# Gated layer: output weights made during its first half, products in another order, and the channel stage's operands and weights loaded one step ahead

## The chip, the cores and the metric

The kernel runs on one core of one Trainium2 chip. The metric is the device time of one execution in microseconds (us), as the median of several runs.

## The reference, cut to what matters

Three layers follow one another, all in float32: attention over 4 batches of 12 heads (448 positions, 64 channels a head), a gated layer (768 to 1024 channels and back), and a mixer that works first over the positions (448 to 256 and back) and then over the channels (768 to 1536 and back).

```python
scores = cap * np.tanh(scale * np.matmul(q, k.transpose(0, 1, 3, 2)) / cap)
attn = np.exp(scores - max); attn = attn / (attn.sum(-1) + 1e-09); x = np.matmul(attn, v)
...
h = np.maximum(x @ w_in, 0.0)                       # gated layer, 768 -> 1024
conv = sum(conv_w[k] * hp[:, k:k + S, :] for k in range(3))
x = h * (1 / (1 + np.exp(-conv))) @ w_out           # 1024 -> 768
...
h = np.maximum(x.transpose(0, 2, 1) @ w_tok1, 0.0) @ w_tok2
u = x + h.transpose(0, 2, 1)
out = u + np.maximum(u @ w_ch1, 0.0) @ w_ch2        # 768 -> 1536 -> 768
```

## The kernel before

Nearly every matrix product is made of three TensorE passes: each float32 operand is split into a rounded high part and the low rest (a cast on ScalarE and a subtraction on VectorE), and `split3` pairs high with high, high with low and low with high. The weights come as float64 words; `narrow` loads such words into `w_raw`, turns them into float32 (one ScalarE pass, three VectorE passes in `w_pt`) and splits them. All transfers are issued on one queue, that of SyncE (SP).

A list scheduler orders each engine's instructions by priority, which is the order of the program text moved by the offsets of `later(...)`, and puts a wait where an instruction needs one; each engine then works through its list in that order. A tile of a pool is taken over when all users of the tile that had its place are done.

**Attention and gated layer.** The loop over `gi` makes one quarter of a head pair's attention at a time. From the second batch on, the gated layer of the batch before is woven in: `gated(b)` is a generator, and each of its `yield`s names a cost that is charged against a budget (`RATES`). Its first half makes, for each of 8 blocks `m`, 18 products with `win[m]` (L466), then the gate on ScalarE and VectorE (L469 to L481), which leaves `gs[m] = (gh, gl)`. Its second half makes, for each of 6 output blocks `m`, 24 products over 8 values of `k` (L492) with the weight tile `wo[b, m]`, evacuates them (L496) and writes `y_d`. `wo` has two buffers of 1 MB. For the first batch (b = 0) `make_wo` narrows each tile from the words in three pieces (L352 to L366) and keeps a copy in `wo_d` (L427); for the other three, `load_wo` reads that copy in one transfer (L435). Here `load_wo(b, 0)` and `load_wo(b, 1)` stand at the start of the second half, and `load_wo(b, m + 1)` at the start of block `m`. One `w_raw` and one `w_pt` buffer of the pool `st` serve, one piece after another, `w_in` (16 pieces), then `w_out` (18 pieces), then `w_ch2` (24 pieces, L504).

**Tokens.** `tokens(b)` transposes `y_d` (L701), splits it (L703 to L707), makes the products over the positions (L718, L732), adds (L734) and writes `u_d` (L735). The steps of batches 0 to 2 are woven into the last batch's `gated`; the rest runs in a loop of its own, `while toks`.

**Channels.** The product `u @ w_ch1` is made by a Strassen-like scheme of seven products a unit (`up`, L873), whose right-hand operands `u0` to `u6` (`BORDER`) are sums and differences of four tiles of `u_d`, split again (L790, L791; the subtractions are L798). `u_make(p, k, want)` loads four tiles (L795) and makes those operands whose names are in `want`. For the first pair of batches, `u_all(0, BORDER[0:3])` makes three kinds during `while toks`, every second step; the other four kinds are made after that loop, from the same tiles loaded again. A step's four loads stand directly ahead of what uses them. The left-hand operands come from `w_ch1` blocks, one for each `wc_step`: `block` loads the words and narrows them at once (L635). `down` makes the second product (L911) with `w2` tiles, of which two lie in the pool `Gm` and two in `Gb`; `Gb` is opened when the tokens' pools are closed.

Of the kernel before, what the change touches and what calls it, by code (L numbers as in the profile page):

```python
# [20 lines left out]
KD = DM // 128  # L21
# [12 lines left out]
W_IN = 5  # L34
W_OUT = 7
# [13 lines left out]
WCK = 3  # L49
RATES = 13.0, 11.5, 13.0, 12.0  # L50
# [253 lines left out]
def fused_kernel(ctx, tc, ins, out, attention):  # L304
# [154 lines left out]
    def gated(b):  # L459
        gs = []  # L460
        for m in range(MF):
            hi, lo = win[m]
            ps = ps_m.tile([128, 512], F32, name="mm")
            for k in range(KD):
                for n, (w, v) in enumerate(split3(hi[:, k], lo[:, k], *X[b, k])):
                    nc.tensor.matmul(ps[:, 0:S], w, v, start=k == 0 and n == 0, stop=k == KD - 1 and n == 2)  # L466
                if k % 2 and k < KD - 1:
                    yield W_IN
# [13 lines left out]
            yield W_IN  # L482
        load_wo(b, 0)
        for m in range(KD):
            if m + 1 < KD:
                load_wo(b, m + 1)
            w = wo.pop((b, m)).rearrange("p t (k n) -> p t k n", n=128)
            hi, lo = w[:, 0], w[:, 1]
            ps = ps_m.tile([128, 512], F32, name="mm")
            for k in range(MF):  # L490
                for n, (w, v) in enumerate(split3(hi[:, k], lo[:, k], *gs[k])):
                    nc.tensor.matmul(ps[:, 0:S], w, v, start=k == 0 and n == 0, stop=k == MF - 1 and n == 2)  # L492
# [135 lines left out]
    def block(pools, src, name):  # L628
# [3 lines left out]
        raw = raw()  # L632
        p = pool.tile([128, 2, 384], U32, name="w_pt")[:, 0]
        t = blk.tile([128, 384], U32, name=name)
        nc.sync.dma_start(raw.rearrange("p n t -> p (n t)"), src)  # L635
# [3 lines left out]
    def unit_jobs(u):  # L639
# [9 lines left out]
        def a11(pools):  # L649
            T["a"] = block(pools, src(0, 0), "ba")  # L650
            put("A11", T["a"])

        def a21(pools):
            T["b"] = block(pools, src(1, 0), "bb")
# [4 lines left out]
        def a22(pools):  # L659
            t = block(pools, src(1, 1), "bx")  # L660
# [7 lines left out]
        def a12(pools):  # L668
            t = block(pools, src(0, 1), "bx")
# [4 lines left out]
        return [a11, a21, a22, a12]  # L674
# [94 lines left out]
    Gb = None  # L769

    def u_tile(o, k):
        name = BORDER[o]
        if o < 3:
            t = Gm.tile([128, 2, S], F32R, name=f"u{o}{k}", tag=f"u{o}{k}")
        elif name == "T4":
            t = Gb.tile([128, 2, S], F32R, name=f"u{o}{k}", tag=f"u{o}{k}")
# [247 lines left out]
```

## Time and profile before

| | |
|---|---|
| runs | 903.06 us median of 3 (899.55 to 904.08) |
| profiled execution | 902.45 us, its span 900.6 us |
| TensorE busy | 867.5 us, 96% of the span |
| VectorE, ScalarE busy | 696.1 and 495.5 us (77% and 55%) |
| granted TensorE clock, mean | 0.991 of full |

The span runs from the first to the last instruction of the profiled execution; the 1.85 us beside it lie around it. A TensorE instruction can overlap the next, so its busy time counts from the start of one to the end of a run of them; idle time stands in brackets or after a bar, with the instruction or transfer that ended it.

### The profile page before, as it was taken

The numbers are of one execution on the slowest core, as the hardware profiler recorded it, in microseconds if no ns is written. First come the engines' busy times: TensorE is split into PE (matmuls) and PEld (weight loads), VectorE is DVE, ScalarE is ACT, GpSimd is POOL, SyncE is SP. The second block draws the span as 40 slices with busy tenths as digits, with TensorE's granted clock in tenths as the row PEclk, the third lists the DMA queues.
The fourth block names the chain that finished last, engine by engine and source line by source line (L and its number), as shares of the span: only waits on it lengthen the run. The fifth ranks groups of instructions, "written<-read, shape, count | busy, mean of one in ns | idle before, by whom it ended". The sixth has DMA issues, their size and how long they took to land.

```text
span 900.6 us, 12120 instructions
## 1 busy us (share of the span) xinstructions
PE 867.5 (96%) x4105; PEld 754.4 (84%) x4105; DVE 696.1 (77%) x1271; ACT 495.5 (55%) x820; POOL 4.7 (1%) x19
## 2 busy tenths in 40 slices
PE   8999999989989999999999998999999999999997
PEld 4665887868978889888989988789989899999996
DVE  7889987789997899956897576796967859478342
ACT  6889888767886779863764243442423423143110
POOL 0000000000000000000000000000000000000000
PEclk9999999999999999999999999999999999999999
DMA  7875564667557864457658766556473744517234
GB/s 277 268 219 171 170 201 147 208 210 243 162 177 265 283 219 145 132 181 263 219 162 258 245 199 199 157 176 195 123 245 96 224 151 126 182 55 224 76 109 140
DMA packets 81719, 168.91 MB, mean 188 GB/s; under 512 B 12050, under 2 KB 57586, under 8 KB 79346
## 3 DMA queue, kind: packets, MB, share of 16 engines
q1 hardware_dynamic: 81650, 168.07, 58.1%
q8 instruction: 34, 0.56, 0.3%
q14 instruction: 35, 0.29, 0.1%
HBM read 126.58 MB, written 38.54 MB: 183 GB/s over the span
## 4 chain that ended last, share of the span: by engine, by line
PE 54%; DVE 19%; DMA 15%; ACT 7%; issue 4%; SPq 1%; POOL 0%; DVEq 0%; ACTq 0%; POOLq 0%
PE mm L911 18%; PE o L873 14%; PE mm L492 9%; DMA w_raw<-in_w_in 3%; DMA w_raw<-in_w_out 2%; DMA c<-u_d 2%; PE mm L466 2%; PE ps_e L718 2%; PE ps_e L732 2%; DMA w_d<-w_pt 1%; DVE ab L115 1%; DMA raw<-in_qk 1%; PE ps_s L147 1%; DVE w_pt L358 1%; PE ps_s L146 1%
## 5 line engine op out<-in xcount | busy, mean ns | idle before, releaser
L911 PE MATMUL mm<-hs,w 128*128 128x448 f32 x864 | 178.4, 367 | 0.8 <-DVE rr L912 0.7
L911 PEld LDWEIGHTS mm<-hs,w 128*128 128x128 f32 x864 | 161.7, 188 | 16.2 <-DVE rr L912 1.4
L492 PE MATMUL mm<-gh,wo 128*128 128x448 f32 x384 | 127.1, 374 | 6.4 <-ACT wo L362 3.4
L466 PE MATMUL mm<-xx,wi_h 128*128 128x448 f32 x384 | 114.7, 370 | 0.2 <-DVE xx L453 0.2
L492 PEld LDWEIGHTS mm<-gh,wo 128*128 128x128 f32 x384 | 72.8, 190 | 17.2 <-ACT wo L362 5.4
L146 PE MATMUL ps_s<-ab 128*128 128x448 f32 x192 | 81.6, 426 | 2.9 <-DVE ab L115 2.1
L466 PEld LDWEIGHTS mm<-xx,wi_h 128*128 128x128 f32 x384 | 71.7, 188 | 9.2 <-issue 1.9
L168 ACT ACTIVATE a<-ps_s,icap 128x896 f32<-128x896 f32 x76 | 67.0, 885 | 22.4 <-PE ps_s L147 17.9
L492 PE MATMUL mm<-gl,wo 128*128 128x448 f32 x192 | 71.2, 371 | 0.4 <-DVE gl L481 0.4
L147 PE MATMUL ps_s<-low,ab 128*128 128x448 f32 x192 | 71.3, 373 | 0.3 <-DVE low L116 0.3
L169 ACT ACTIVATE a<-a,cap 128x896 f32<-128x896 f32 x76 | 70.4, 926 | 1.3
L466 PE MATMUL mm<-xx,wi_l 128*128 128x448 f32 x192 | 70.3, 366 | 0.0
L176 DVE TENSOR_TENSOR al<-a,ah 128x896 fp32r<-128x896 f32 (+1 forms) x56 | 54.3, 971 | 1.7
L873 PE MATMUL o<-u,wi_h 128*128 128x448 f32 x216 | 49.4, 363 | 1.4 <-ACT u L790 1.1
L790 ACT CAST u<-c 128x448 fp32r<-128x448 f32 x48 | 27.0, 567 | 42.5 <-DVE c L798 21.9
L873 PE MATMUL o<-u,wi_l 128*128 128x448 f32 x216 | 47.9, 362 | 0.0
L146 PEld LDWEIGHTS ps_s<-ab 128*128 128x128 f32 x192 | 36.3, 190 | 13.4 <-issue 5.0
L175 DVE CAST ah<-a 128x896 fp32r<-128x896 f32 (+1 forms) x56 | 31.5, 565 | 18.9 <-PE ob L196 9.6
L873 PEld LDWEIGHTS o<-u,wi_h 128*128 128x128 f32 x216 | 40.5, 188 | 5.1 <-ACT u L790 1.9
L147 PEld LDWEIGHTS ps_s<-low,ab 128*128 128x128 f32 x192 | 36.4, 190 | 9.0 <-issue 5.4
L873 PEld LDWEIGHTS o<-u,wi_l 128*128 128x128 f32 x216 | 40.5, 187 | 2.7
L111 ACT CAST ab<-raw 128x960 fp32r<-128x960 f32 x36 | 35.4, 992 | 12.3 <-DMA raw<-in_qk 7.1
(166 smaller groups left out, 1690.5 us busy)
## 6 DMA issues: line engine op xcount, KB each, us to landing
wo<-wo_d SPq DMA_DIRECT2D x18, 1024.0 KB
raw<-in_qk SPq DMA_DIRECT2D x18, 960.0 KB
w_raw<-in_w_ch SPq DMA_DIRECT2D x40, 384.0 KB
c<-u_d SPq DMA_DIRECT2D x60, 224.0 KB
w_raw<-in_w_in SPq DMA_DIRECT2D x16, 384.0 KB
e<-in_qk SPq DMA_DIRECT2D x6, 960.0 KB
y_d<-c SPq DMA_DIRECT2D x24, 224.0 KB
yt<-y_d SPq DMA_DIRECT2D x24, 224.0 KB
```

The lines of the kernel that those rows point to most:

```text
L111: nc.scalar.copy(h, r)
L146: nc.tensor.matmul(ps[:, bank, 0:S], a[:, keys], a[:, 0:S], start=start, stop=False)
L147: nc.tensor.matmul(ps[:, bank, 0:S], a[:, keys], low, start=False, stop=stop)
L168: nc.scalar.activation(a[:, 0:n], ps[:, 0:n, 0:S], AF.Tanh, scale=self.c["icap"])
L169: nc.scalar.activation(a[:, 0:n], a[:, 0:n], AF.Exp, scale=self.c["cap"])
L175: nc.vector.tensor_copy(ah[:, 0:n], a[:, 0:n])
L176: nc.vector.tensor_tensor(al[:, 0:n], a[:, 0:n], ah[:, 0:n].bitcast(F32), op=ALU.subtract)
L466: nc.tensor.matmul(ps[:, 0:S], w, v, start=k == 0 and n == 0, stop=k == KD - 1 and n == 2)
L492: nc.tensor.matmul(ps[:, 0:S], w, v, start=k == 0 and n == 0, stop=k == MF - 1 and n == 2)
L790: nc.scalar.copy(w[:, 0], t)
L873: nc.tensor.matmul(ps, l, r, start=k == 0 and n == 0, stop=k == 2 and n == 2)
L911: nc.tensor.matmul(ps[:, 0:S], l, x, start=r == 0 and n == 0, stop=r == 3 and n == 2)
```

## The change

The second half's first two weight tiles are asked for at blocks 5 and 7 of the first half, in every batch; each later tile `m + 2` is asked for when block `m` is done. For the three later batches the first two output blocks are made together: `k` = 0 to 6 of block 0, `k` = 0 to 6 of block 1, and then `k` = 7 of both. For the first batch the yields cost 4 in the first half and 8 in the second, where all batches had 5 and 7; the sum of a batch's yields stays 288. In the channel stage, `u_begin` makes the first pair's operands in two groups (four kinds, then three) with each step's four loads issued one step earlier, alternately into the tiles `c` and into four tiles that are idle by then (`temp`); the first group runs at odd steps below 20 of `while toks`, the second from step 17 of the last batch's tokens on. T3 moves to `Gm`, T4 to the pool `xe`, and all four `w2` tiles to `Gb`. `wc_step` issues the words of the next `w_ch1` block before it narrows this one. `up` takes its four temporaries at once, in another order.

```diff
-W_IN = 5
-W_OUT = 7
+PACE = (4, 8), (5, 7)
+WO_AT = 5, 7
+UB_AT = 20, 17
...
     def gated(b):
         gs = []
+        w_in, w_out = PACE[b > 0]
         for m in range(MF):
+            if m in WO_AT:
+                load_wo(b, WO_AT.index(m))
...
-        load_wo(b, 0)
-        for m in range(KD):
-            if m + 1 < KD:
-                load_wo(b, m + 1)
-            w = wo.pop((b, m)).rearrange("p t (k n) -> p t k n", n=128)
...
-                if k % 2 and k < MF - 1:
-                    yield W_OUT
+        def mm(m, k):
+            if k == 0:
+                acc[m] = ps_m.tile([128, 512], F32, name="mm")
+            w = wo[b, m].rearrange("p t (k n) -> p t k n", n=128)
+            for n, (l, v) in enumerate(split3(w[:, 0, k], w[:, 1, k], *gs[k])):
+                nc.tensor.matmul(acc[m][:, 0:S], l, v, start=k == 0 and n == 0, stop=k == MF - 1 and n == 2)
+
+        def done(m):
+            del wo[b, m]
             y = cv_p.tile([128, S], F32, name="c", bufs=4)
-            nc.scalar.activation(y, ps[:, 0:S], AF.Copy, scale=0.5)
+            nc.scalar.activation(y, acc.pop(m)[:, 0:S], AF.Copy, scale=0.5)
             nc.sync.dma_start(y_d[b, m], y)
-            yield W_OUT
+            if m + 2 < KD:
+                load_wo(b, m + 2)
+
+        blocks = [[(0, k) for k in range(MF - 1)] + [(1, k) for k in range(MF - 1)] + [(0, MF - 1), (1, MF - 1)]] if b else [[(m, k) for k in range(MF)] for m in range(2)]
+        blocks += [[(m, k) for k in range(MF)] for m in range(2, KD)]
+        n = 0
+        for m, k in (i for l in blocks for i in l):
+            mm(m, k)
+            if k == MF - 1:
+                done(m)
+            n += 1
+            if n % 2 == 0:
+                yield w_out
...
     def wc_step(pools, n=1):
         for _ in range(n):
             if todo:
                 with later(tc, O_NA):
-                    todo.pop(0)(pools)
+                    for words, _ in todo[len(ahead) : 2]:
+                        ahead.append(fetch(pools, words))
+                    todo.pop(0)[1](ahead.pop(0))
...
+    def u_first(k, b11, b12, b22, b21):
+        u_put(k, "B11", b11)
+        sub(b11, b12, b11)
+        yield
+        sub(b12, b22, b12)
+        sub(b22, b22, b11)
+        u_put(k, "T2", b22)
+        yield
+        u_put(k, "B21", b21)
+        u_put(k, "T3", b12)
+        yield
+
+    def u_rest(k, b11, b12, b22, b21):
+        sub(b11, b12, b11)
+        sub(b12, b22, b11)
+        sub(b21, b12, b21)
+        u_put(k, "T4", b21)
+        yield
+        u_put(k, "T1", b11)
+        u_put(k, "B22", b22)
+        yield
+
+    def u_begin():
+        steps = [(u, i) for u in (u_first, u_rest) for i in range(3)]
+        ts = u_load(0, 0, 0)
+        yield
+        for n, (u, i) in enumerate(steps):
+            coming = u_load(0, steps[n + 1][1], (n + 1) % 2) if n < 5 else None
+            yield from u(i, *ts)
+            ts = coming
...
-        if k % 2:
-            next(first, None)
+        n += 1
+        left += len(toks) == 1
+        if n % 2 and n < UB_AT[0] or left >= UB_AT[1]:
+            next(begin, None)
...
-        pool = Gm if c % 4 < 2 else Gb
-        w2[c] = w = pool.tile([128, 2, KD * 128], F32R, name=f"w2_{c % 4}", tag=f"w2_{c % 4}")
+        w2[c] = w = Gb.tile([128, 2, KD * 128], F32R, name=f"w2_{c % 4}", tag=f"w2_{c % 4}")
...
-        p1, u2 = temp(), temp()
+        p1, c21, u3, u2 = (temp() for _ in range(4))
...
-    for _ in u_all(0, BORDER[3:7]):
-        pass
```

## Rows read from the trace of the kernel before

**Rows 1.** The page: engines over the span, and the longest group of products.

```profile
PE 867.5 (96%) x4105; PEld 754.4 (84%) x4105; DVE 696.1 (77%) x1271; ACT 495.5 (55%) x820; POOL 4.7 (1%) x19
L911 PE MATMUL mm<-hs,w 128*128 128x448 f32 x864 | 178.4, 367 | 0.8 <-DVE rr L912 0.7
```

**Rows 2.** TensorE's groups from 176 to 216 us, idle time and releasers last.

```profile
L492 PE MATMUL mm<-gh,wo 128*128 128x448 f32 x35 | 12.1, 386 | 4.2 <-ACT wo L362 3.4 <-DVE wo L366 0.7
```

**Rows 3.** TensorE in order of time, first batch: first and last of three waits.

```profile
179.36 0.47 PE L492 MATMUL mm<-gh,wo 128*128 128x448 f32 x1 [1.38 <-ACT wo L362]
...
212.02 0.47 PE L492 MATMUL mm<-gh,wo 128*128 128x448 f32 x1 [1.01 <-ACT wo L362]
```

**Rows 4.** All users of `wo`: min/median/max ns, first and last start in us.

```profile
L492 PE MATMUL mm<-gh,wo x384: 358/367/742, 138.7 to 522.7; 128*128 128x448 f32 x192
...
L362 ACT CAST wo<-w_pt x18: 396/502/517, 110.4 to 218.0; 128x384 fp32r<-128x384 f32 x12, 128x256 fp32r<-128x256 f32 x6
```

**Rows 5.** Transfers of `w_out` pieces in order of time on SP: first, eighth, ninth.

```profile
99.63 0.33 SPq L352 DMA_DIRECT2D w_raw<-in_w_out  x1
...
143.18 0.33 SPq L352 DMA_DIRECT2D w_raw<-in_w_out  x1
...
153.72 0.33 SPq L352 DMA_DIRECT2D w_raw<-in_w_out  x1
```

**Rows 6.** TensorE's waits over the span: us in total, times, longest.

```profile
PE mm L492 <- ACT gh L480: 1.2, 2, 1.1
```

**Rows 7.** TensorE in order of time around the second batch's turn.

```profile
260.73 0.36 PE L492 MATMUL mm<-gh,wo 128*128 128x448 f32 x1
...
268.42 0.47 PE L197 MATMUL oa<-al,v 128*128 128x448 f32 x1 [1.42 <-DVE al L176]
269.97 0.74 PE L492 MATMUL mm<-gh,wo 128*128 128x448 f32 x1 [1.08 <-ACT gh L480]
```

**Rows 8.** SP, ACT and PE in order of time, last batch's tokens.

```profile
542.98 9.94 SPq L795 DMA_DIRECT2D c<-u_d  x8
...
547.09 0.56 ACT L790 CAST u<-c 128x448 fp32r<-128x448 f32 x1 [1.87 <-DMA c<-u_d]
...
548.08 0.62 PE L718 MATMUL ps_e<-xx,wt 128*128 128x384 f32 x2 [2.73 <-ACT xx L703]
```

**Rows 9.** PE and DVE in order of time, start of the channel stage.

```profile
560.02 1.97 PE L873 MATMUL o<-u,wi_h 128*128 128x448 f32 x9
...
565.16 0.62 DVE L798 TENSOR_TENSOR c<-c 128x448 f32<-128x448 f32 x1 [3.30 <-DMA c<-u_d]
```

**Rows 10.** TensorE's groups from 552 to 575 us, idle time and releasers last.

```profile
L873 PE MATMUL o<-u,wi_h 128*128 128x448 f32 x23 | 6.0, 372 | 1.0 <-ACT u L790 0.8 <-DVE u L791 0.3
L873 PE MATMUL o<-xx,wi_l 128*128 128x448 f32 x12 | 4.1, 479 | 1.2 <-ACT xx L790 1.2
```

**Rows 11.** By stretch: window, length, engines' busy us, clock, DMA share, GB/s.

```profile
80.00:140.00 60.00, 59.51 (x251) 46.30 (x250) 53.19 (x104) 52.14 (x86) 1.96 (x6) 1.00 0.54 173
180.00:200.00 20.00, 17.21 (x73) 13.87 (x73) 18.00 (x30) 13.26 (x21) 0.63 (x1) 0.91 0.60 194
260.00:280.00 20.00, 17.50 (x78) 15.06 (x77) 16.24 (x29) 15.53 (x24) 0.00 (x0) 0.91 0.63 204
284.00:304.00 20.00, 20.00 (x100) 18.01 (x99) 15.37 (x26) 15.83 (x23) 0.00 (x0) 1.00 0.83 292
560.00:580.00 20.00, 17.79 (x78) 15.56 (x78) 14.60 (x26) 7.40 (x14) 0.00 (x0) 0.91 0.55 170
```

**Rows 12.** SP in order of time: the second batch's second weight tile.

```profile
226.88 0.33 SPq L435 DMA_DIRECT2D wo<-wo_d  x1
```

**Rows 13.** The chain that ended last, at the end of the third batch.

```profile
410.76 5.77 DMA wo<-wo_d
```

**Rows 14.** TensorE's groups from 284 to 304 us.

```profile
L492 PE MATMUL mm<-gh,wo 128*128 128x448 f32 x37 | 12.1, 366 | 0.0
L492 PE MATMUL mm<-gl,wo 128*128 128x448 f32 x19 | 6.9, 364 | 0.0
```

More of the change, by code (lines that the diff above doesn't have):

```diff
@@ L467, in gated @@
                 if k % 2 and k < KD - 1:
-                    yield W_IN
+                    yield w_in
             h = hb[m % 2]
@@ L481, in gated @@
             nc.vector.tensor_tensor(gl, c, gh.bitcast(F32), op=ALU.subtract)
[L482 to L494 removed]
+            yield w_in
+        acc = {}
+        def mm(m, k):
[6 more added lines that the diff above has]
+            del wo[b, m]
             y = cv_p.tile([128, S], F32, name="c", bufs=4)
[L496 removed]
+            nc.scalar.activation(y, acc.pop(m)[:, 0:S], AF.Copy, scale=0.5)
             nc.sync.dma_start(y_d[b, m], y)
[L498 removed]
+            if m + 2 < KD:
[10 more added lines that the diff above has]
+                yield w_out
     def w2_early(c, i):
@@ L806, in u_make @@
         yield
-        if "T3" in want:
-            sub(b12, b22, b12)
-            put("T3", b12)
-        sub(b22, b22, b11)
-        put("T2", b22)
-        yield
-        if "T4" in want:
-            sub(b21, b22, b21)
-            put("T4", b21)
-        yield
-    def u_all(p, want):
-        for k in range(3):
-            yield from u_make(p, k, want)
+        u_put(k, "B21", b21)
[10 more added lines that the diff above has]
+        yield
@@ new lines, in u_begin, with u_all @@
+    def u_begin():
[6 more added lines that the diff above has]
+            ts = coming
+    def u_all(p):
+        for k in range(3):
+            b11, b12, b22, b21 = u_load(p, k)
+            u_put(k, "B11", b11)
+            sub(b11, b12, b11)
+            u_put(k, "T1", b11)
+            yield
+            u_put(k, "B21", b21)
+            u_put(k, "B22", b22)
+            yield
+            sub(b12, b22, b12)
+            u_put(k, "T3", b12)
+            sub(b22, b22, b11)
+            u_put(k, "T2", b22)
+            yield
+            sub(b21, b22, b21)
+            u_put(k, "T4", b21)
+            yield
@@ L822, in fused_kernel, with temp @@
+    spare = [0]
+    def temp():
+        spare[0] = i = (spare[0] + 1) % 4
+        if i < 2:
+            return cv_p.tile([128, S + 2], F32, name=f"h{i}", tag=f"h{i}")[:, 0:S]
+        name = ("sums", "rr")[i - 2]
+        return pools["sm"].tile([128, S], F32, name=name, tag=name)
     toks.append(tokens(B - 1))
-    first = u_all(0, BORDER[0:3])
+    begin = u_begin()
+    n = left = 0
     while toks:
@@ L829, in fused_kernel @@
             wc_step(st_pools)
-        if k % 2:
-            next(first, None)
-    for _ in first:
+        n += 1
+        left += len(toks) == 1
+        if n % 2 and n < UB_AT[0] or left >= UB_AT[1]:
+            next(begin, None)
+    for _ in begin:
         pass
```

74 lines of the change are left out of this document (32 added, 42 removed).

## The prediction

> **What bounds the kernel now.** I read the page first: TensorE is busy for 867.5 us, 96% of the span, the next engine for 77% [rows 1]. So the change can give back only what TensorE stands idle, and what its clock loses after standing. Second come its waits and its groups by stretch, which say where it stands; third the timelines of the queue or engine named there, which say why. What the reader should see are three places.
>
> The first is the first batch's second half. In 40 us L492 stands 4.2 us, all of it for pieces of `wo` still being narrowed [rows 2], at three points of the same look, 14 to 18 us apart (the middle one is left out) [rows 3]. The pieces were not asked for late: the first was cast at 110.4 us and the first product ran at 138.7 [rows 4]. They come through one `w_raw` and one `w_pt` buffer. The 18 transfers start at 99.63; the ninth starts 10.5 us after the eighth, where those before came every 6.2 us ((143.18 - 99.63) / 7) [rows 5]. The tile they fill takes the place of tile 0, whose products are running then. So this chain, not the program's order, is what is late.
>
> The second is the turn in the later batches: L492 waited for the last gate block 1.2 us in all, 1.1 of it once [rows 6], at 269.97, just after an attention wait of 1.42 [rows 7].
>
> The third is the end of the tokens. Eight loads of `u_d` drag over 9.94 us on SP, ScalarE reaches a cast of theirs 1.87 us before its load lands, the tokens' own copies stand behind that cast, and TensorE stands 2.73 us [rows 8]. Then three products' worth of operands are ready and the fourth's are not: VectorE waits 3.30 us for another load [rows 9], and L873 stands 1.0 and 1.2 us [rows 10].
>
> The clock adds to each: 0.91 over the 20 us of 180 to 200, 260 to 280 and 560 to 580, 1.00 in the other stretches shown [rows 11]. Either level is 2.4 or 1.2 GHz, so each of these stretches lost 20 x (1 - 0.91) = 1.8 us, each after waits of over 2 us within a few us.
>
> **Operands one step ahead.** The number of loads (24), casts (21) and VectorE passes stays; only their place moves. Each step's four loads stand a whole step (three calls) before their use, so the cast no longer meets its own load, and the copies behind it go through. T3 joins the first group: four products instead of three are ready at the start, 9 passes more at 0.20 us (100 in 20 us) [rows 11], 1.8 us of cover, and the second group begins while the tokens' last products run. What goes: 2.73 + 1.0 + 1.2 and the dip after it, 1.8: 6.7 us. Bounds: 0 (the casts still block) to 6.7. I take it whole, as the waits named are on the loads themselves and on what queued behind them. VectorE has room for it (14.6 of 20 us) [rows 11]. What is late next is T4 and T1 in `xe`, whose nine places the tokens' copies hold until their last block; the 1.8 us of cover is theirs.
>
> **First batch.** The change lets `load_wo(0, 0)` and `(0, 1)` with all their work (six transfers in, six out, 12 ScalarE and 24 VectorE passes) stand at an earlier place, and moves a later tile by one yield. The transfers in cannot start before 99.63, because `w_in` has the buffers until then; but the passes get their turn sooner, and the pace (4 for 5, then 8 for 7) brings tile 0 to its end sooner, so the 10.5 us gap, 4.3 over the others, shrinks; and it spreads the second half over 192 / 168 of the steps. Against this, block 5 is needed earlier too. Bounds of the gain: 0, and 4.2 + 1.8 = 6.0 us. I take half, 3.0, since the chain gains some 4 us and loses part of it to the earlier need. The pace has a bound on the other side: in 80 to 140 VectorE carries 53.2 of 60 us [rows 11]; squeezed by a fifth throughout, that work would be 53.2 - 48 = 5.2 us late. Only the gate's part is squeezed, and the attention of the steps left out goes with it, so I put nothing and keep 5 us for the range.
>
> Of the rule that repeated gaps can mean too few buffers (the Trainium skill, Perfetto Trace Analysis, Identifying the Most-Contended Engine and Optimization Strategy), this trace gives an instance, three gaps of one kind in 33 us [rows 3], and the change adds no buffer. By the rule the first batch would give 0 instead of 3.0; that is the second rival below.
>
> **Later batches, first two tiles.** Asked for sooner, but the second batch's second tile is issued at 226.88 [rows 12], and its first product runs at 260.73 [rows 7]: 33.8 us of slack hide an earlier or later issue. A transfer of 1 MB takes 5.77 us [rows 13]. So 0 here; if that cover were gone, 5.8. SP's other transfers stand behind such an issue when it waits for its place; the same slack pays.
>
> **Later batches, new order.** With block 1 between, the last gate block has 21 more passes to arrive, 4.3 us; the 1.2 us of [rows 6] go. The dip at 270 follows 1.42 and 1.08 us of waiting; one of these goes, so I count half of 1.8. Together 2.1; bounds 0 and 3.0.
>
> **Its cost.** Tile 2 takes tile 0's place. Before, it was asked for with all of block 1 to run. Now block 0 ends three passes (0.6 us) before block 1, and block 2 comes at once: of 5.77 us, 5.2 are bare in each of three batches, and tile 3 is in flight beside it. What can cover them is attention. At 284 to 304 us 56 of 100 passes are L492's [rows 14], 44 attention's, and ScalarE is busy 15.83 of 20 [rows 11], so attention could run at most 20 / 15.83 = 1.26 times as fast and fill 0.44 x 1.26 = 0.55 of the time. That leaves 0.45 x 5.2 = 2.3 us. Bounds: 0, when the scheduler finds enough, and 3 x (5.2 + 1.8) = 21.0, all bare and a dip each. I take 2.3 in the second and third batch and nothing in the fourth, where three batches' token products stand ready: 4.6 us.
>
> For 1 MB the Trainium skill (DMA: Bandwidth & Descriptors, Bandwidth) has 6.15 us, measured on another issuing path; the row here has 5.77. By the page the bare time would be 5.55 and the term 5.0, a sum later by 0.4.
>
> **At nothing.** Words one block ahead: the transfers feed `up`, and in the whole of L911's 178.4 us TensorE idles 0.8 [rows 1]. The temporaries' order: within the same 0.8. `w2` in `Gb`: first used after two `up`s, 126 passes or 25 us. If these covers fail, what is lost is at most a late transfer, as the 5.77.
>
> **Sum.** 902.45 (span 900.6 and 1.85 around it) - 6.7 - 3.0 - 2.1 + 4.6 = 895.2. The runs' median, 903.06, is 0.6 above the profiled execution, so 895.9; I say 896.
>
> **Rivals.**
> *The pair's loads stand bare.* Place: the start of block 2 in three batches. For it: block 0 now frees its place 0.6 us before the need. Against it: other ready products can stand in TensorE's list ahead of block 2, as attention's L197 stands between L492's at the second batch's turn [rows 7]. At full price 902.45 - 11.8 + 21.0 = 911.7, with the 0.6 912. It decides from 11.8 / 3 = 3.9 us a batch on; at that it is level. This is the case that ends slower.
> *The first batch's chain stays late.* Same buffers, same start at 99.63. 902.45 - 6.7 - 2.1 + 4.6 = 898.3, or 899; up to 904 if VectorE falls behind by 5. The Trainium skill's rule on repeated gaps, weighed above, would give this time.
> *The casts stay in the way.* The loads lie ahead, but the first group's casts are denser (12 in ten steps, not 9 in twelve), and ScalarE and SP still serve in order; TensorE stands in the same place. Against it: the wait shown is on a load, not on ScalarE's load (7.4 of 20 us) [rows 11]. 902.45 - 3.0 - 2.1 + 4.6 = 902.0, or 902.6.
> All gains and no cost would be 902.45 - 6.7 - 6.0 - 3.0 = 886.8, or 887.
>
> **How the numbers follow.** The three runs spread by 0.5%, so less than that, 4.5 us, cannot be told from no change: faster is below 898.5, slower above 907.6. The forecast gets 0.52, its own range 887 to 900 (0.47 faster, 0.05 same). Bare loads: 0.18 (0.06 same, 0.12 slower). Late chain: 0.17 (0.07 faster, 0.10 same). Casts: 0.13 (0.11 same, 0.02 slower). Together 0.54 faster, 0.32 same, 0.14 slower. The range for 8 in 10 goes from all gains, 886, to short of the bare loads' full price, 908.
>
> **What would show it.** Operands: no wait of L718 near 548 nor of L873 near 567, no VectorE wait on `c<-u_d`, and clock 1.00 where 0.91 stood. First batch: waits of L492 on L362 below 2 us. Order: no wait on L480, and in its place L492 waiting on DMA `wo<-wo_d` at block 2 of the second and third batch, over 2 us each. The prediction is wrong if these DMA waits sum to more than 12 us, if attention's waits (L197) grow in the first batch, or if ScalarE's copies L703 still end a TensorE wait of 2 us.

## Result and profile after

The changed kernel is slower: 909.96 us (median of 12 runs, 905.86 to 914.86) beside 902.71 us (12 runs, 898.49 to 906.45) for the kernel before, a ratio of 1.0082 with a 95% interval of 1.0055 to 1.0108, or 7.3 us more, where the forecast's sum had 7.2 us less (902.45 to 895.2). The profiled execution took 912.74 us, its span 910.7.

The page of the kernel after: its engines, and the group of the last products, which answer to [rows 1].

```profile
PE 870.6 (96%) x4105; PEld 752.7 (83%) x4105; DVE 695.0 (76%) x1271; ACT 494.5 (54%) x820; POOL 3.9 (0%) x19
...
L969 PE MATMUL mm<-hs,w 128*128 128x448 f32 x864 | 179.7, 367 | 2.9 <-DVE rr L970 1.8
```

No engine does more work than before. What grew is waiting. TensorE's waits of the kernel after (us in total, times, longest), which answer to [rows 6]:

```profile
PE mm L494 <- DMA wo<-wo_d: 5.9, 4, 2.2
PE mm L494 <- ACT wo L363: 5.9, 4, 2.2
...
PE ps_e L744 <- DVE xx L731: 2.2, 2, 1.9
...
PE ob L196 <- DVE ah L176: 1.9, 1, 1.9
PE mm L969 <- DVE rr L970: 1.8, 4, 0.7
```

Before, the first two were 1.0 and 3.4 us. The waits on the last gate block (then L480, now L484) are gone, as are those on L790 and L791 at the start of the channel stage [rows 10].

The two profiled spans differ by 10.1 us. Where this arises can be read from the time at which the n-th TensorE instruction starts (both kernels have 4105). The first line of the table has these starts in the kernel before; under it stands what the kernel after adds to each stretch, in us, worked out from the starts of both:

| stretch of TensorE instructions | to 1050th: first batch | to 2250th: later batches | to 2580th: start of the channel stage | to the last: channels |
|---|---|---|---|---|
| ends at, before | 265.8 | 513.9 | 583.5 | 894.3 |
| after | +4.6 | +9.1 | -6.5 | +3.0 |

**First batch.** TensorE in order of time and SP in order of time (transfers of `w_out` pieces: first, eighth, ninth, last) of the kernel after, then all users of `wo`; they answer to [rows 3 to 5].

```profile
183.11 0.47 PE L494 MATMUL mm<-gh,wo 128*128 128x448 f32 x1 [2.20 <-ACT wo L363]
...
198.55 0.48 PE L196 MATMUL ob<-ah,v 128*128 128x448 f32 x1 [1.94 <-DVE ah L176]
...
204.19 0.48 PE L494 MATMUL mm<-gh,wo 128*128 128x448 f32 x1 [1.66 <-ACT wo L363]
```

```profile
103.44 0.33 SPq L353 DMA_DIRECT2D w_raw<-in_w_out  x1
...
147.22 0.33 SPq L353 DMA_DIRECT2D w_raw<-in_w_out  x1
152.04 0.33 SPq L353 DMA_DIRECT2D w_raw<-in_w_out  x1
...
210.01 0.33 SPq L353 DMA_DIRECT2D w_raw<-in_w_out  x1
```

```profile
L363 ACT CAST wo<-w_pt x18: 389/508/519, 113.1 to 215.8; 128x384 fp32r<-128x384 f32 x12, 128x256 fp32r<-128x256 f32 x6
```

The last of these transfers in the kernel before:

```profile
209.88 0.33 SPq L352 DMA_DIRECT2D w_raw<-in_w_out  x1
```

The gap ahead of the ninth piece is gone (4.8 us, it was 10.5). But the last piece is asked for at 210.01, where it was 209.88: the chain starts 3.8 us later, and its pieces come every (210.01 - 103.44) / 17 = 6.3 us, where they came every 6.5. What TensorE gained ahead of this chain it waits for inside it.

The stretches of the kernel after (window, length, busy us of PE, PEld, DVE, ACT and POOL, clock, DMA share, GB/s), which answer to [rows 11]:

```profile
140.00:160.00 20.00, 20.00 (x96) 17.38 (x95) 16.61 (x32) 16.34 (x26) 0.82 (x3) 1.00 0.59 196
...
180.00:200.00 20.00, 15.51 (x64) 12.16 (x63) 17.60 (x30) 13.19 (x21) 0.48 (x1) 0.91 0.53 179
200.00:220.00 20.00, 15.89 (x73) 12.48 (x72) 17.54 (x33) 14.62 (x25) 0.00 (x0) 1.00 0.79 258
260.00:280.00 20.00, 19.42 (x94) 16.81 (x93) 18.32 (x33) 16.89 (x27) 0.00 (x0) 1.00 0.50 158
...
280.00:300.00 20.00, 17.75 (x81) 15.15 (x80) 12.06 (x21) 11.50 (x17) 0.00 (x0) 0.94 0.79 275
...
410.00:430.00 20.00, 17.63 (x85) 15.13 (x84) 9.76 (x18) 4.97 (x10) 0.00 (x0) 1.00 0.68 219
...
560.00:580.00 20.00, 19.69 (x103) 18.00 (x102) 16.78 (x32) 8.33 (x16) 0.00 (x0) 1.00 0.62 197
```

TensorE is full from 140 to 160 and stands for 8.6 of the 40 us from 180 to 220. The clock dips of before at 260 to 280 and 560 to 580 are gone, the one at 180 to 200 is still there; there is a new one behind the wait at 297.

**Second batch.** TensorE and SP in order of time in the kernel after, and three transfers of `wo` in its chain of work that ended last; they answer to [rows 7, 12, 13].

```profile
286.75 0.36 PE L196 MATMUL oa<-ah,v 128*128 128x448 f32 x1
...
287.76 0.37 PE L494 MATMUL mm<-gh,wo 128*128 128x448 f32 x1
...
294.34 0.37 PE L198 MATMUL ob<-al,v 128*128 128x448 f32 x1
296.81 0.47 PE L494 MATMUL mm<-gh,wo 128*128 128x448 f32 x1 [2.10 <-DMA wo<-wo_d]
```

```profile
282.48 0.32 SPq L436 DMA_DIRECT2D wo<-wo_d  x1
286.88 0.32 SPq L522 DMA_DIRECT2D w_d<-w_pt  x1
...
287.77 0.88 SPq L500 DMA_DIRECT2D y_d<-c  x2
288.70 0.50 SPq L436 DMA_DIRECT2D wo<-wo_d  x1
```

```profile
288.70 8.07 DMA wo<-wo_d
...
399.70 5.67 DMA wo<-wo_d
...
489.69 7.20 DMA wo<-wo_d
```

The pair's last products ran at 282.9. Tile 2, asked for at 282.48, was waited for by nobody: attention alone filled TensorE from the pair's end up to 287.76, when block 2 began. Tile 3 is what came late. Its request stood on SP behind a store of `w_d` that waited for its data until 286.88 and behind two stores of `y_d`, so it went out at 288.70, 5.8 us after the pair; it took 8.07 us, and block 3 stood 2.10 us. In the third batch tile 2 took 5.67 us and was nearly covered too, and the wait (2.23 us, at 421.20) came two blocks later, on tile 4; in the fourth batch tile 2's 7.20 us ended in a wait of 1.25 us at 496.93.

### The profile page after: what moved, and what is told of

Its sections match the earlier page's. It is cut to its first block, busy times and chain, and to the rows that moved or that the text cites. A ratio compares the mean times of both kernels' runs of the same rounds, so it can differ in the third digit from the quotient of the medians.

```text
span 910.7 us, 12133 instructions
## 1 busy us (share of the span) xinstructions
PE 870.6 (96%) x4105; PEld 752.7 (83%) x4105; DVE 695.0 (76%) x1271; ACT 494.5 (54%) x820; POOL 3.9 (0%) x19
## 4 chain that ended last, share of the span: by engine, by line
PE 51%; DMA 20%; DVE 18%; ACT 7%; issue 4%; SPq 0%; ACTq 0%; DVEq 0%
PE o L931 16%; PE mm L969 15%; PE mm L494 6%; DMA c<-u_d 4%; PE mm L470 4%; DMA w_raw<-in_w_tok 3%; DMA w_raw<-in_w_in 3%; DMA w_raw<-in_w_out 3%; DMA wo<-wo_d 2%; DMA raw<-in_qk 2%; DMA w_raw<-in_w_ch 2%; PE ps_e L744 2%; PE ps_e L758 2%; DVE ab L116 1%; DVE w_pt L359 1%
## 5 line engine op out<-in xcount | busy, mean ns | idle before, releaser
L969 PE MATMUL mm<-hs,w 128*128 128x448 f32 x864 | 179.7, 367 | 2.9 <-DVE rr L970 1.8
L969 PEld LDWEIGHTS mm<-hs,w 128*128 128x128 f32 x864 | 161.6, 188 | 20.0 <-DVE rr L970 3.3
L931 PE MATMUL o<-u,wi_h 128*128 128x448 f32 x216 | 47.1, 362 | 0.0
L819 ACT CAST u<-c 128x448 fp32r<-128x448 f32 x44 | 24.3, 565 | 35.3 <-DMA c<-u_d 21.5
L744 PE MATMUL ps_e<-xx,wt 128*128 128x384 f32 x176 | 36.0, 344 | 4.0 <-DVE xx L731 2.2
## 6 DMA issues: line engine op xcount, KB each, us to landing
c<-u_d SPq DMA_DIRECT2D x48, 224.0 KB
y_d<-c SPq DMA_DIRECT2D x24, 224.0 KB
yt<-y_d SPq DMA_DIRECT2D x24, 224.0 KB
```

What stands on the lines that cost most here:

```text
L744: nc.tensor.matmul(ps[:, 0:384], l, r, start=c == 0 and n == 0, stop=c == NS - 1 and n == 1)
L819: nc.scalar.copy(w[:, 0], t)
L931: nc.tensor.matmul(ps, l, r, start=k == 0 and n == 0, stop=k == 2 and n == 2)
L969: nc.tensor.matmul(ps[:, 0:S], l, x, start=r == 0 and n == 0, stop=r == 3 and n == 2)
```

## Experiments

All ratios are to the kernel before on the same chip in the same rounds (its median was between 904.32 and 906.02 us), with a 95% interval; a ratio need not be the quotient of two medians. Runs of one kernel spread by some 0.6% to either side, so one profiled execution says where time went, and only the ratio says how much.

**One part alone.** The channel part with the gated layer of before, and the reverse.

```diff
+UB_AT = 20, 17
...
-        pool = Gm if c % 4 < 2 else Gb
...
-        p1, u2 = temp(), temp()
+        p1, c21, u3, u2 = (temp() for _ in range(4))
...
-    for _ in u_all(0, BORDER[3:7]):
-        pass
```

> The channel stage's part alone (operands and words one step ahead, w2 in Gb, temporaries in the new order); the gated layer as before. The trace of the changed kernel regains 6.7 us of its arrears between matmul 2400 and 2600, and loses 3.2 us by matmul 2800, in down. Theory A (the gated part costs, the channel part gains): 3.5 to 6.7 us under the kernel before, ratio 0.993 to 0.996. Rival C (the channel part is what costs, by its waits in down): ratio 1.003 or more.

Measured: 904.28 us, ratio 0.9992 (0.9964 to 1.0019), between theory A and rival C.

```diff
-W_IN = 5
-W_OUT = 7
+PACE = (4, 8), (5, 7)
+WO_AT = 5, 7
```

> The gated layer's part alone (weights at blocks 5 and 7, new order, new pace); the channel stage as before. Theory A: the change's 7.4 us plus what the channel part gains, 11 to 14 us over the kernel before, ratio 1.012 to 1.016. Rival C: ratio 1.005 or less.

Measured: 914.1 us, ratio 1.0103 (1.0067 to 1.0138). The whole loss lies in the gated part, about 9.3 us (0.0103 x 906), and the channel part alone gives nothing that can be told from zero: theory A has the loss, smaller than it said, and not the gain.

**After, without the pair, and with the old pace.**

```diff
-        blocks = [[(0, k) for k in range(MF - 1)] + [(1, k) ... if b else [[(m, k) for k in range(MF)] for m in range(2)]
+        blocks = [[(m, k) for k in range(MF)] for m in range(2)]
```

> The changed kernel with blocks 0 and 1 one after the other in all batches. Theory A1 (of the gated part it is the pair's order that costs, as the weights of block 2 are asked for too late; L494 waits 5.9 us on wo in the changed kernel, 1.0 before): 5 to 8 us under the changed kernel, ratio to the kernel before 0.999 to 1.003. Rival A2 (the pace and the early weights of the first batch cost): the ratio stays at 1.006 to 1.010.

Measured: 909.8 us, ratio 1.0041 (1.0013 to 1.007), between theory A1 and rival A2.

```diff
-PACE = (4, 8), (5, 7)
+PACE = (5, 7), (5, 7)
```

> The changed kernel with the first batch's yields at 5 and 7 again. Theory A1: 0 to 3 us under the changed kernel, ratio 1.005 to 1.008. Rival A2: ratio 1.001 or less.

Measured: 910.04 us, ratio 1.0057 (1.0028 to 1.0086), as theory A1 has it. Taken out of the whole change, the pair is worth 1.0082 - 1.0041, or 3.7 us, and the pace 2.3 us; the intervals overlap.

**Each edit of the gated part on the kernel before.** The early request alone, the pair alone, the pace alone, and early request and pace in the first batch only. In all of them but the pace alone each later tile is also asked for at the end of a block, not at the start of the next, in the first batch too; this was not tried by itself.

```diff
+            if m in WO_AT:
+                load_wo(b, WO_AT.index(m))
...
-        load_wo(b, 0)
```

> Before, with the first two weight tiles asked for at blocks 5 and 7 of the first half in every batch; order, pace and channel stage as before. Theory P (the pair's order is what costs, the early request costs nothing): 901 to 906 us, ratio 0.997 to 1.002, TensorE's waits on the casts of wo at most the 3.4 us of before, and waits on wo<-wo_d near 0 to 1. Rival F (the first batch's second half got worse by the early request): 907 to 911 us, ratio 1.003 to 1.007, waits on the casts of wo 4.5 to 6 us.

Measured: 909.23 us, ratio 1.0022 (0.9988 to 1.0056), which decides nothing; the waits on the casts of `wo` were 3.5 us, those on `wo<-wo_d` 2.3.

```diff
         load_wo(b, 0)
-        for m in range(KD):
-            if m + 1 < KD:
-                load_wo(b, m + 1)
...
+        load_wo(b, 1)
...
+        blocks = [[(0, k) for k in range(MF - 1)] + [(1, k) for k in range(MF - 1)] + [(0, MF - 1), (1, MF - 1)]] if b else [[(m, k) for k in range(MF)] for m in range(2)]
```

> Before, with the first two output blocks of the three later batches made together; the request for the weights stays at the start of the second half. Theory P: 907 to 911 us, ratio 1.004 to 1.008, TensorE waits on wo<-wo_d of 1 to 2.5 us at block 2 of each later batch, 5 to 6 us in all. Rival F: the pair costs at most 2 us, ratio 0.999 to 1.002, the waits on wo<-wo_d below 3 us in all.

Measured: 917.57 us, ratio 1.0127 (1.0084 to 1.017), the dearest of all and beyond theory P's range; the waits on `wo<-wo_d` came to 5.7 us, as in the kernel after.

```diff
-W_IN = 5
-W_OUT = 7
+PACE = (4, 8), (5, 7)
```

> Before, with the first batch's yields at 4 and 8 in place of 5 and 7. Theory P: no difference, 900 to 905 us, ratio 0.997 to 1.001. Rival F: the second half's blocks come with the chain no further on, so the waits on the casts of wo grow from 3.4 to 4.5 to 6 us: 905 to 909 us, ratio 1.002 to 1.005.

Measured: 905.49 us, ratio 0.9984 (0.9953 to 1.0015): no difference, although the waits on the casts grew from 3.4 to 5.1 us.

```diff
+        w_in, w_out = PACE[b > 0]
...
+            if b == 0 and m in WO_AT:
+                load_wo(b, WO_AT.index(m))
...
+        if b:
+            load_wo(b, 0)
+            load_wo(b, 1)
```

> Before, with the early request and the pace of 4 and 8 in the first batch alone; the later batches and the channel stage as before. Theory P: 901 to 905 us, ratio 0.997 to 1.001. Rival F: 907 to 912 us, ratio 1.004 to 1.008, waits on the casts of wo 5 to 6 us, and the lead of before 4 to 6 us at the 900th TensorE instruction.

Measured: 909.79 us, ratio 1.0044 (1.0018 to 1.0069). Neither theory stands alone: the pair costs, and so does the first batch, where the early request and the pace cost together (some 4 us) what neither costs alone.

**Ending block 0 sooner.** The kernel with the pair alone, still interleaved, but block 0 gets its last products after two values of k of block 1.

```diff
-[(0, k) for k in range(MF - 1)] + [(1, k) for k in range(MF - 1)] + [(0, MF - 1), (1, MF - 1)]
+[(0, k) for k in range(MF - 1)] + [(1, 0), (1, 1), (0, MF - 1)] + [(1, k) for k in range(2, MF)]
```

> Before, with the first two output blocks of the later batches still interleaved, but block 0 given its last products after two values of k of block 1, so that 18 products of block 1, not 3, follow the end of block 0. Both accumulators are still held over most of the pair. Theory T (the pair costs because tile 0 frees its place too late): 900 to 907 us, ratio 0.997 to 1.002, TensorE's waits on wo<-wo_d at most 2 us in all, none on gh. Rival H (the pair costs by holding two accumulators or by its order as such): 910 to 918 us, ratio 1.006 to 1.013.

Measured: 915.08 us, ratio 1.0109 (1.008 to 1.0138): theory T missed, and the time is where rival H had it. SP and TensorE in order of time, third batch of this kernel:

```profile
411.06 0.44 SPq L434 DMA_DIRECT2D wo<-wo_d  x1
```

```profile
415.11 0.37 PE L492 MATMUL mm<-gh,wo 128*128 128x448 f32 x1
418.63 0.44 PE L492 MATMUL mm<-gh,wo 128*128 128x448 f32 x1 [3.16 <-DMA wo<-wo_d]
```

This is the only wait on a tile in this kernel: tile 2 now came in time in every batch, and tile 4 of the third did not: asked for at 411.06, it was there at 418.6, 7.5 us later, while block 3 was through at 415.5.

**A third place for `wo`.** Both leave out the low part of the gate's result, which frees the memory; the second has three places.

```diff
-            gl = g_p.tile([128, S], F32R, name="gl", bufs=8)
-            gs.append((gh, gl))
+            gs.append((gh, gh))
...
-            nc.vector.tensor_tensor(gl, c, gh.bitcast(F32), op=ALU.subtract)
```

> After, without the low part of the gate's result: its subtraction is left out and the high part stands in its place in the products, whose number stays. wo keeps two places. The memory this frees is used by the next kernel only. 905 to 911 us, ratio 1.002 to 1.008, TensorE's waits on wo<-wo_d 4 to 7 us as in after.

Measured: 908.89 us, ratio 1.0014 (0.9981 to 1.0047), just below what was expected.

```diff
-        wo[b, m] = wo_p.tile([128, 2, MF * 128], F32R, name="wo", bufs=2)
+        wo[b, m] = wo_p.tile([128, 2, MF * 128], F32R, name="wo", bufs=3)
...
+        load_wo(b, 2)
...
-            if m + 2 < KD:
-                load_wo(b, m + 2)
+            if m + 3 < KD:
+                load_wo(b, m + 3)
```

> The same without the low part, with three places for wo: the third tile is asked for at the second half's start, each later tile m + 3 when block m is done. Theory T (the pair's price is tiles that come late because their places come free late): waits on wo<-wo_d at most 1 us, the stretch from the 1050th to the 2250th TensorE instruction 4 to 7 us shorter than with two places, the time 4 to 7 us below it. Rival H (the order as such, or the two accumulators held): that stretch within 2 us of the one with two places, and the time too.

Measured: 906.89 us, ratio 1.0014 (0.9984 to 1.0045). From the 1050th to the 2250th TensorE instruction the two take +5.1 and +5.3 us over the kernel before. The waits on `wo<-wo_d` (4.9 us with two places) are gone with three, and the time is not. TensorE in order of time in the kernel with three places, at the ends of the second and the third batch:

```profile
321.56 0.47 PE L452 MATMUL mm<-rr,sel 128*128 128x448 f32 x1 [0.91 <-DVE xx L454]
322.63 0.96 PE L470 MATMUL mm<-xx,wi_h 128*128 128x448 f32 x2 [0.60 <-DVE xx L454]
```

```profile
420.93 0.44 PE L452 MATMUL mm<-rr,sel 128*128 128x448 f32 x1 [2.10 <-DVE rr L447]
```

In place of the tile, TensorE waits for the chain that normalizes the next batch (4.2 us in this stretch, 0.7 with two places); the clock is 0.91 in 310 to 330 and in 410 to 430, where it was 1.00 and 0.91 with two. Theory T falls as the whole account of the pair, and rival H's figures hold; H names the order and the two accumulators, and no run tells these apart.

**The first batch's chain, lighter and longer.** Lighter: two of the three VectorE passes that turn a `w_out` piece into float32 left out, in the kernel before and in the one after; `light` is set for `w_out` alone.

```diff
-        nc.vector.scalar_tensor_tensor(out=t, in0=raw[:, :, 0], scalar=29, in1=t, op0=ALU.logical_shift_right, op1=ALU.bitwise_or)
-        nc.vector.scalar_tensor_tensor(out=t, in0=p, scalar=0x80000000, in1=t, op0=ALU.bitwise_and, op1=ALU.bitwise_or)
+        if not light:
+            nc.vector.scalar_tensor_tensor(out=t, in0=raw[:, :, 0], scalar=29, in1=t, op0=ALU.logical_shift_right, op1=ALU.bitwise_or)
+        if not light:
+            nc.vector.scalar_tensor_tensor(out=t, in0=p, scalar=0x80000000, in1=t, op0=ALU.bitwise_and, op1=ALU.bitwise_or)
```

> Before, with two of the three VectorE passes left out that turn a piece of w_out into float32 (sign and lowest bits are lost). Theory F (in the first batch the narrowing of the pieces sets the end of the second half, before and after alike): TensorE's waits on the casts of wo fall from 3.4 to below 1 us, 896 to 901 us, ratio 0.991 to 0.997. Rival O (the first batch's loss lies in the attention's own waits): the waits on the casts may go, but the time stays within 0.3%.

Measured: 894.11 us, ratio 0.9852 (0.9813 to 0.9891), more than theory F had; one wait of 1.7 us on a cast of `wo` is left.

> After, with the same two passes left out. Theory F: waits on the casts of wo below 1 us; the stretch from the 600th to the 1050th TensorE instruction comes back by 4 us or more, the time is 901 to 905 us, ratio 0.997 to 1.002: what is left over the lightened kernel before is the pair's price less the channel part's gain. Rival O: 906 to 911 us, ratio 1.004 to 1.009.

Measured: 903.84 us, ratio 0.9966 (0.9938 to 0.9993). Up to the 1050th TensorE instruction the two stand at -7.6 and -6.2 us to the kernel before, where the kernels with the whole chain stood at 0 and +4.6: most of the first batch's loss goes with the chain. Most of what is left between them, 9.7 us, is in the later batches (-2.5 and +7.1).

Longer: the last pass of each piece moved from VectorE to GpSimd, nothing left out, on the kernel before and together with the channel part with all its loads a step ahead (the last kernel of the next group).

```diff
-            nc.vector.tensor_tensor(dst[1], t, dst[0].bitcast(F32), op=ALU.subtract)
+            (low or nc.vector).tensor_tensor(dst[1], t, dst[0].bitcast(F32), op=ALU.subtract)
...
-        narrow(st_p, 384, wide["w_out"][m, :, 2 * lo : 2 * hi], (t[:, 0], t[:, 1]))
+        narrow(st_p, 384, wide["w_out"][m, :, 2 * lo : 2 * hi], (t[:, 0], t[:, 1]), low=nc.gpsimd)
```

> Before, with the last pass of each of the 18 pieces of w_out (the subtraction that gives the low part, 0.51 us on VectorE) issued on GpSimd; nothing is left out. Theory V (VectorE's load makes the pieces late and the attention's copies with them): 18 x 0.51 = 9 us less for VectorE, waits on the casts of wo below 2 us, 897 to 902 us, ratio 0.991 to 0.998. Rival S (the piece's own chain through one buffer sets it, and a pass on GpSimd takes longer than on VectorE): waits on the casts as before or longer, 903 to 910 us, ratio 0.999 to 1.006.

Measured: 912.86 us, ratio 1.0072 (1.0042 to 1.0102).

> The channel part with all operand loads one step ahead, and the low parts of w_out on GpSimd: the version that the experiments point to. Theory V: 895 to 901 us, ratio 0.989 to 0.997, below both kernels. Rival S: 902 to 909 us, ratio 0.998 to 1.005.

Measured: 909.23 us, ratio 1.0035 (1.0005 to 1.0066). The rival held in direction, in the first kernel by more than its range: 18 passes of 9.2 us left VectorE, and the kernel got slower. The subtraction of the larger pieces in the kernel before and in the first of these:

```profile
L366 DVE TENSOR_TENSOR wo<-w_pt,wo 128x384 fp32r<-128x384 f32 x12 | 6.7, 555 | 2.0 <-ACT wo L362 1.7
```

```profile
L366 POOL TENSOR_TENSOR wo<-w_pt,wo 128x384 fp32r<-128x384 f32 x12 | 13.0, 1079 | 95.9 <-ACT wo L362 95.9
```

VectorE's busy time did not fall, though: it is 696.0 us for 696.1, because its other passes took longer, 5.7 us in sum. One group from 95 to 225 us, in the kernel before and in this one:

```profile
L176 DVE TENSOR_TENSOR al<-a,ah 128x896 fp32r<-128x896 f32 x13 | 14.1, 1087 | 0.4
```

```profile
L176 DVE TENSOR_TENSOR al<-a,ah 128x896 fp32r<-128x896 f32 x14 | 18.1, 1294 | 0.8
```

So these runs show what a longer chain costs at an unchanged VectorE busy time; a lighter VectorE with the chain as it was has not been tried. The casts of `wo` in the first kernel and in the lightened kernel before (first and last start behind the comma):

```profile
L362 ACT CAST wo<-w_pt x18: 390/502/517, 110.5 to 224.0; 128x384 fp32r<-128x384 f32 x12, 128x256 fp32r<-128x256 f32 x6
```

```profile
L364 ACT CAST wo<-w_pt x18: 393/503/516, 106.3 to 200.1; 128x384 fp32r<-128x384 f32 x12, 128x256 fp32r<-128x256 f32 x6
```

The last cast, at 218.0 in the kernel before [rows 4], moves to 224.0 and to 200.1; by the ratios the time moves by +6.5 and -13.4 us. The chain of pieces sets when the first batch can end.

**What the channel part gives back.** The channel part alone, with one further edit each: the temporaries in the old order, the `w_ch1` words not ahead, and the second pair's operand loads one step earlier too.

```diff
-        p1, c21, u3, u2 = (temp() for _ in range(4))
+        p1, u2 = temp(), temp()
...
+        u3, c21 = temp(), temp()
```

> The channel part alone, with the four temporaries of each unit taken in the order of before. Theory D (what is given back in the second product comes from the operand loads that stand directly ahead of their use): as the channel part alone, 900 to 906 us, ratio 0.996 to 1.002, and the stretch from the 2580th TensorE instruction on still 2 to 5 us longer than before. Rival E (the other order of the temporaries delays the adds): that stretch within 1.5 us of before, 897 to 902 us, ratio 0.993 to 0.998.

Measured: 906.19 us, ratio 1.0007 (0.9983 to 1.0032); the last stretch +5.6 us.

```diff
-                    for words, _ in todo[len(ahead) : 2]:
-                        ahead.append(fetch(pools, words))
+                    ahead.append(fetch(pools, todo[0][0]))
```

> The channel part alone, with each w_ch1 block's words asked for directly ahead of their use, as before. Theory D: as the channel part alone, ratio 0.996 to 1.002, the stretch from the 2580th TensorE instruction on 2 to 5 us longer than before. Rival G (the words asked for one block ahead stand in the way of the operand loads): that stretch within 1.5 us of before, ratio 0.993 to 0.998.

Measured: 904.78 us, ratio 0.9999 (0.9968 to 1.0029); the last stretch +2.9 us.

```diff
     def u_all(p):
+        ts = u_load(p, 0)
+        yield
         for k in range(3):
-            b11, b12, b22, b21 = u_load(p, k)
+            b11, b12, b22, b21 = ts
...
+            if k < 2:
+                ts = u_load(p, k + 1)
             yield
...
         coming = u_all(np_) if np_ != p else iter(())
+        next(coming, None)
```

> The channel part alone, with the second pair's operand loads of each step asked for one step earlier too, so that no load stands directly ahead of its use. Theory D: the waits of the second product on the add (L955 in the channel part alone) go to about 1 us in all, the stretch from the 2580th TensorE instruction on is within 1.5 us of before, 896 to 902 us, ratio 0.992 to 0.998. Rivals E and G: as the channel part alone, ratio 0.996 to 1.002.

Measured: 903.31 us, ratio 0.9982 (0.9955 to 1.001); the last stretch +3.5 us. None of the three brings that stretch back to within 1.5 us, so theories D, E and G all miss. The kernels without the channel part spread from 0 to +3.3 there (next table), so +2.9 and +3.5 alone would not tell. ScalarE, VectorE and TensorE in order of time in the channel part alone show one instance for D:

```profile
830.27 0.57 ACT L804 CAST u<-c 128x448 fp32r<-128x448 f32 x1 [1.97 <-DMA c<-u_d]
```

```profile
830.87 0.63 DVE L805 TENSOR_TENSOR u<-c,u 128x448 fp32r<-128x448 f32 x1 [1.91 <-ACT u L804]
831.42 1.28 DVE L807 TENSOR_TENSOR c<-c 128x448 f32<-128x448 f32 x2
832.61 0.62 DVE L955 TENSOR_TENSOR rr<-mm,rr 128x448 f32<-128x448 f32 x1
```

```profile
833.28 2.08 PE L954 MATMUL mm<-hs,w 128*128 128x448 f32 x5 [2.73 <-DVE rr L955]
```

The cast meets its own load, VectorE waits for the cast, the add that frees TensorE's accumulator stands behind both. With the loads a step earlier the waits on that add fall from 5.0 to 2.8 us, but the kernel before had 0.7.

**All kernels together.** The stretches of the first table, to the kernel before, one profiled execution each (us):

| kernel | first batch | later batches | start of channels | channels |
|---|---|---|---|---|
| after | +4.6 | +9.1 | -6.5 | +3.0 |
| gated part alone | +3.0 | +7.9 | -0.5 | +0.9 |
| after, old pace | +0.7 | +9.4 | -6.3 | +3.7 |
| pair alone | +5.4 | +8.0 | -1.3 | +2.5 |
| block 0 sooner | +2.6 | +7.5 | -0.4 | +1.0 |
| after, plain order | +2.2 | +2.3 | -6.0 | +2.8 |
| early request alone | +1.0 | +3.4 | -1.4 | +1.0 |
| pace alone | -1.3 | +3.4 | -1.3 | +3.3 |
| first batch's edits | +3.4 | +1.1 | -2.8 | +2.0 |
| channel part alone | +1.9 | +3.0 | -6.4 | +6.8 |
| old temporaries | +0.1 | +5.5 | -6.4 | +5.6 |
| words not ahead | +0.2 | +3.3 | -5.3 | +2.9 |
| second pair ahead | +2.5 | -1.0 | -6.2 | +3.5 |
| GpSimd pass | +6.0 | +4.6 | -2.2 | +1.1 |
| GpSimd pass, second pair ahead | +5.0 | +2.6 | -6.4 | +4.5 |

All of these do the whole work. Means over them and the kernel before: later batches +8.4 with the pair (5 kernels, 7.5 to 9.4), +2.6 without (11, -1.0 to 5.5), so the pair costs 5.8. Start of channels -6.2 with the channel part (8), -1.2 without (8); behind it +4.1 and +1.5, with ranges that overlap (2.8 to 6.8, 0 to 3.3): a gain of 5.0 of which 2.6 is given back. First batch +3.3 with early request and pace together (4), +1.3 without them both and without the GpSimd pass (10, -1.3 to 5.4): a loss of 2.0, no larger than that spread. The sum, 5.8 - 5.0 + 2.6 + 2.0 = 5.4 us, lies inside what was timed for the whole change (0.0055 to 0.0108 of 902.7, 5.0 to 9.7).

No kernel that does the whole computation beats the one before by more than its interval; the fastest, with the second pair's loads ahead as well, is 1% below the kernel after (0.9982 / 1.0082 = 0.990).

## Why the prediction was wrong

By the means of the last section the first batch came out 5.0 us worse than forecast (-3.0, +2.0), the new order with its cost 3.3 (+2.5, +5.8), the edits put at nothing 2.6, and the operands 1.7 (-6.7, -5.0): 12.6 of the 14.5 us between -7.2 and +7.3.

**Operands one step ahead: right in its place, not in its sum.** No wait of 2 us on the copies (then L703), none on the operands, no dip at 560 to 580, and -6.5 us in that stretch where -6.7 was said. Two things took it back. The kernel profiled before had been unlucky there by about 1.2 us, as the other kernels without the edit show. And the step "at nothing", whose cover was L911's 0.8 us of idle time, was wrong: its waits grew (now L969, 2.9 us), and the stretch by 2.6 us in the mean. Four kernels with this part and the gated layer of before have a mean ratio of 0.9995, so it is worth at most one or two us. What delays the adds stays open: neither the temporaries' order nor the words ahead, undone alone, removed it, and moving the loads removed it in part. The new places of T3, T4 and `w2` were not tried alone.

**First batch: the step that failed.** It said -3.0, because "the chain gains some 4 us and loses part of it to the earlier need". The gap did shrink, by 5.7 us, and TensorE was 3.5 us ahead of the kernel before at its 550th instruction, counted from the 300th. But this lead came back as waits: those on the casts went from 3.4 to 5.9 us, where "below 2 us" had been the sign of success, and attention waited 1.94 us at 198.55. (The clock dip in 180 to 200 of the kernel before followed waits of 1.4 and 0.3 us, not of over 2 as the prediction reads it.) What the working left out is how far the need itself moves. The chain's last cast is only 2.1 us sooner, but the products that wait for it are now TensorE's 789th to 794th instructions, where they were the 817th to the 822nd. The first of them in the kernel before and in the kernel after, each 0.05 us behind the end of that cast:

```profile
218.42 0.47 PE L492 MATMUL mm<-gh,wo 128*128 128x448 f32 x1
```

```profile
216.29 0.47 PE L494 MATMUL mm<-gh,wo 128*128 128x448 f32 x1 [1.17 <-ACT wo L363]
```

So 28 instructions at 0.20 us, 5.6 us of work that had run ahead of the chain's end, now stand behind it. Less the 2.1 us, that is 3.5 of the +4.6. The same two figures, the end of the last cast and the place of its first product, give the start of the 1050th instruction to within 1.3 us in every kernel here. The place is 829 with the early request, 822 with the pace and 789 with both, so the two cost together what neither costs alone: the first batch's edits took 4.0 us (0.0044 x 905.9). Why the scheduler puts it there no run shows. The second rival, the chain stays late, named the place and the chain; its 899 us had the first batch at no change, and it was a loss.

The bound put on VectorE ("up to 904 if VectorE falls behind by 5") looked at another thing: with 9.2 us of passes taken from VectorE, its busy time unchanged and each piece some 0.5 us longer, the kernel lost 6.5 us. The rule that repeated gaps of one kind can mean too few buffers (the Trainium skill, Perfetto Trace Analysis, Optimization Strategy), which the prediction weighed and gave the smaller chance, pointed at the one pair of buffers. The runs with a lighter and a longer chain agree with it as far as they go; a second buffer itself was not tried.

**Later batches, first two tiles: right.** Asked for at 211.01 and 224.27 instead of 207.54 and 226.88, and not waited for. The cover was larger than said: the product at 260.73 is block 0's, and block 1 began at 273.6.

**New order: right.** The waits on the last gate block are gone, and the kernel after gains 3.4 us between the 1050th and the 1100th instruction where 2.1 was said.

**Its cost: right in its kind, wrong in place and size.** Waits of 4.6 us were said, 5.9 came. Block 2's tile, which the working was about, was covered by attention, fully in the second batch and to 0.34 us in the third. What it missed: the wait turns up one or two blocks later instead; tile 3's request stands on SP behind a store that waits for its data; and with other transfers issued just ahead 1 MB took 7.2 to 8.1 us, not 5.77. For 1 MB the Trainium skill (DMA: Bandwidth & Descriptors, Bandwidth) has 6.15 us, measured on another issuing path, which lies between the shorter transfers here (5.67, 5.77) and the longer ones. The fourth batch, put at nothing, waited 1.25 us. The net price of the order, 4.6 - 2.1 = 2.5 in the prediction, is 5.8 by the stretches, 3.7 when taken out of the change and 11.5 (0.0127 x 905.9) when put in alone. So the first rival, bare loads, was nearest by its number, 912 us, but not by its mechanism: it had 21.0 us of bare loads, and the waits sum to 5.9; nor were its 3.9 us a batch reached (5.8 / 3 = 1.9). Such waits come without the pair too, 2.3 us in the kernel after with plain order.

Open remains why the third place for `wo` does not bring the time back. Shown is that the tile's waits go and that waits for the normalizing chain stand in their place; that the pair spends the products which had covered that chain is argued from these rows, not shown by a run of its own, and the kernel after with plain order, which has no pair, waits 1.8 us for that chain as well. Why the pair alone costs three times what it costs within the change is open in part. Its first batch too ends 5.4 us later, though the only edit there is the later tiles' request at a block's end: the last piece's products stand at the 804th place for the 817th.

## What to carry to other kernels

A gain ahead of a serial chain is worth no more than the time by which its last link comes sooner (here 2.1 us after 18 pieces at 6.3), and it is a loss if the work that ran ahead of that link's use now stands behind it (here 28 instructions). So ask when the last link ends and what stands ahead of the products that need it, not how long the waits in its middle are. When work of one kind is to cover a late transfer, ask what that work covered until now, for the wait turns up there. And price a transfer from the moment its queue can issue it, with what is issued just ahead of it.

## What the runs showed of the hardware

A subtraction of 128x384 took 1.08 us on GpSimd and 0.56 us on VectorE in the same place. The Trainium skill (GPSIMD Engine Reference, Performance versus the Vector engine) has a factor of about two for such passes, which this agrees with. Beside it VectorE itself slowed down: of its 42 subtractions of 128x896 in that kernel, the 7 that ran beside one on GpSimd took 1.50 us in the mean, up to 1.89, and the other 35 took 1.09 each. Transfers of 1 MB took between 5.67 and 8.07 us in one execution: the shortest had nothing issued in the 3 us ahead of it, the longest 832 KB in the 1.4 us ahead of it. A wait of 2.10 us brought the granted clock of the 20 us around it to 0.94, and one of 2.23 us at 421.20 in the same execution left it at 1.00 (410 to 430): the dips cannot be counted from the waits alone.
